# Threshold attention feeding a tanh-shrink layer: all queries and the second batch's masks turned on TensorE, first batch's weights three slots sooner

## The chip, the core and the metric

The kernel runs on one core of one Trainium2 chip. A core has five engines that run their own instruction streams and meet at semaphores: TensorE (PE in the profile, with its weight loads as PEld), VectorE (DVE), ScalarE (ACT), GpSimd (POOL) and SyncE (SP), which here only issues DMAs. The metric is the device time of one execution in microseconds.

## The reference

```python
def _attn_ref(q, k, v, tau):            # q, k, v: (8, 8, 576, 64) float32
    scores = matmul(q, k.T) / sqrt(64)
    thresh = max(scores, axis=-1) - tau          # tau = 0.02
    scores = where(scores >= thresh, scores, -1e9)
    attn = exp(scores - max(scores))
    attn = attn / (sum(attn) + 1e-9)
    return matmul(attn, v)
...
x = attn_out.transpose(0, 2, 1, 3).reshape(4608, 512)
h = x @ w_in                             # w_in: (512, 2048)
g = h - tanh(h)
out = g @ w_out                          # w_out: (2048, 512)
```

## The kernel before

**Tiles.** The 64 heads are taken as 32 pairs, four pairs to a batch entry ("batch" below). Each pair has nine score tiles of 128 query rows by 576 keys: kinds A and B (512 rows of each head, two A/B duos a head) and one tile M (j = 4), which holds the last 64 rows of both heads. Tile i is number j = i mod 9 of pair p = i div 9.

**Steps of a pair.** `load` brings k, q and v from DRAM through SP's queue. `split` (GpSimd, three operations) scales q or k by 256 and writes it as a float16 high and low half. `turn` transposes the halves: nine 128x128 transposes on TensorE into one of the two `ps_big` PSUM buffers, and one VectorE copy to SBUF; for k, two GpSimd copies then make the swapped `kS`. In the kernel before, `q_by_dma(p)` sends q of the odd pairs from 9 on (12 of them) through a DMA transpose on SP's queue instead. `split_v` (GpSimd, three casts) fills the value tile `vb`.

**Steps of a tile.** `scores` (four matmuls into `ps_big`, and one VectorE pass L323 that scales, copies and takes the row maximum), `shift` (a small VectorE operation L337 that makes the bias), `kink` (one ScalarE pass L357, a steep Prelu that sends what lies below the threshold far down, output `z`), `weights` (transposes z and takes the exponential, output `pT`), `attend` (matmuls with `vb` into `ps_o`), `norm` (VectorE), `emit_x` (transposes the normalised pair into the layer's input `xT`).

**Two ways to transpose z.** Where `on_pe(i)` holds, `weights` runs four or five 128x128 transposes on TensorE into PSUM (`psZ`) and one exponential per tile (512 or 640 wide, L386). Otherwise `kink` issues a DMA transpose on SP's queue for each finished duo or M tile (L365), into one of the `zt_pool` buffers, and `weights` runs one exponential of 1152 for the duo (L394). Before, TensorE does all tiles of pairs 0 to 3, tiles 0, 1, 4, 5, 6 of pairs 4 to 7, and none after.

**The layer.** `layers` gives the steps of a batch's 512 rows: `hidden` (four 512-wide matmuls, then `bend` = tanh on ScalarE and `shrink` on VectorE) and `project` (four 512-wide matmuls of a quarter of the sum). Steps are dealt out over the slots of the next batch's tiles, from its slot 4 to its last one; slots 0 to 3 of a batch have none. The first stage, over pairs 4 to 7, has 16 hidden steps and no projection; later ones have about one step a slot. The rest runs in a tail after the last tile.

**The order** is written out by hand, one loop over slots s. In slot s stand, in this order: `shift` and `scores` of tile s + AHEAD, `kink` of tile s + MASK, tanh, `weights` of tile s, the layer's steps, `attend` of tile s - LAG (2), `norm`, `emit_x`, and the steps of `PREP`, whose times are counted back from the slot in which a pair's first scores are due (`first = 9 p - AHEAD`). The casts of the layer's weights (16 pieces, GpSimd, L605) stand at every fourth score slot. Each engine keeps this order; the buffers' semaphores do the rest.

Of the kernel before, what the change touches and what calls it, by code (L numbers as in the profile page):

```python
# [9 lines left out]
F32 = mybir.dt.float32  # L10
BF16 = mybir.dt.bfloat16
FP16 = mybir.dt.float16
AX = mybir.AxisListType
ALU = mybir.AluOpType
# [4 lines left out]
def kernel(  # L19
# [11 lines left out]
    nc = tc.nc  # L31
    P = 128

    B, H, S, D = q.shape
# [6 lines left out]
    QKSC = 256.0  # L41
# [4 lines left out]
    HPAIR = H // 2  # L46
# [3 lines left out]
    TPP = 9  # L50
# [3 lines left out]

    def on_pe(i):
        p, j = divmod(i, TPP)
        return p < HPAIR or p < 2 * HPAIR and j in (0, 1, 4, 5, 6)

    W = 2 * S

    AHEAD = 8
    LDK = 16
    MASK = 5
    LAG = 2


# [45 lines left out]
    sc_pool = pool("sc", AHEAD - MASK + 2)  # L112
    st_pool = pool("st", 12)
    z_pool = pool("z", 4)
    zt_pool = pool("zt", 6)
    p_pool = pool("p", 3)
    o_pool = pool("o", 2)
    wt_pool = pool("wt", 2)
# [16 lines left out]
    def load(p, t):  # L135
        b, h0 = p // HPAIR, 2 * (p % HPAIR)
        hs = slice(h0, h0 + 2)
        src = {"k": k, "q": q, "v": v}[t]
        eng = nc.sync
        r = raws[p, t] = raw_pool.tile([P, 10, D], F32, name=f"{t}raw", tag=t)  # L140
        n = 8 if t == "v" else 10
        eng.dma_start(
            out=r[:, 0:n, :].rearrange("p (h c) d -> p h (c d)", h=2)[:, :, 0 : 4 * D],
            in_=src[b, hs, 0:512, :].rearrange("h (p c) d -> p h (c d)", c=4),
        )
        rem = src[b, hs, 512:S, :].rearrange("h s d -> s h d")
        if t == "v":
            eng.dma_start(out=r[0:64, 8:10, :], in_=rem)
        else:
            eng.dma_start(out=r[:, 4, :], in_=rem)  # L150

# [19 lines left out]
    hls = {}  # L171

    def split(p, t):
        x = raws.pop((p, t))[:, 0:9, :]
        hl = hl_pool.tile([P, TPP, 2, D], FP16, name=f"{t}hl", tag=t)
        nc.gpsimd.tensor_scalar(
            out=x, in0=x, scalar1=QKSC, scalar2=1.0, op0=ALU.mult, op1=ALU.mult
        )
        nc.gpsimd.tensor_copy(out=hl[:, :, 0, :], in_=x)
        nc.gpsimd.tensor_tensor(  # L180
            out=hl[:, :, 1, :], in0=x, in1=hl[:, :, 0, :], op=ALU.subtract
        )
        hls[p, t] = hl
# [22 lines left out]
    def split_v(p):  # L206
        r, vb = raws.pop((p, "v")), vbs[p % NV]
        nc.gpsimd.tensor_copy(
            out=vb[:, :, 0:4, 0:D],
            in_=r[:, 0:8, :].rearrange("p (h c) d -> p h c d", h=2),  # L210
        )
        nc.gpsimd.tensor_copy(out=vb[0:64, :, 4, 0:D], in_=r[0:64, 8:10, :])
        nc.gpsimd.tensor_copy(out=vb[64:P, :, 5, 0:D], in_=r[0:64, 8:10, :])

# [11 lines left out]
            out=out, lhsT=lhsT, rhs=rhs, is_transpose=True, start=True, stop=True  # L228
        )

    def q_by_dma(p):

        return p >= 2 * HPAIR and p % 2 == 1

    def turn(p, t):
        hl = hls.pop((p, t))
        if t == "q" and q_by_dma(p):
            m = mats[p, t] = qk_pool.tile([P, W], FP16, name=f"{t}T", tag=t)
            nc.sync.dma_start_transpose(
                out=m.rearrange("p (c r) -> p c r", c=TPP),  # L240
                in_=hl.rearrange("p c a d -> p (c a d)"),
            )
            return
        ps = ps_big.tile([P, W], FP16, name=f"ps_{t}", tag="big")
        for c in range(TPP):
            turn_chunk(
                ps[:, c * P : (c + 1) * P], c, hl[:, c, :, :].rearrange("p a d -> p (a d)")
            )
        m = qk_pool.tile([P, W], FP16, name=f"{t}T", tag=t)
        nc.vector.tensor_copy(out=m, in_=ps)  # L250
        mats[p, t] = m
        if t == "k":
            sw = qk_pool.tile([P, W], FP16, name="kS", tag="ks")
            for lo, hi in ((0, D), (D, 0)):
                o, i = sw[lo : lo + D, :], m[hi : hi + D, :]
                nc.gpsimd.tensor_copy(out=o, in_=i)  # L256
            mats[p, "ks"] = sw
# [31 lines left out]
    def scores(i):  # L289
        p, j = divmod(i, TPP)  # L290
        qT, kT, kS = mats[p, "q"], mats[p, "k"], mats[p, "ks"]
        ps = ps_big.tile([P, 1024], F32, name="psS", tag="big")
        main, rem, lo = slice(0, 512), slice(512, 576), 0
        if kind(j) == "B":
            main, rem, lo = slice(512, 1024), slice(448, 512), 448
        if j == 4:
            qrem = REM
            if q_by_dma(p):
                qrem = (slice(512, 640, 2), slice(513, 640, 2))
            for n, kk in enumerate((kT, kS)):  # L300
                for dst, srcs in ((main, MAIN), (rem, REM)):
                    for hh in range(2):
                        nc.tensor.matmul(  # L303
                            out=ps[64 * hh : 64 * hh + 64, dst],
                            lhsT=qT[:, qrem[hh]], rhs=kk[:, srcs[hh]],
                            start=(n == 0), stop=(n == 1),
                        )
        else:
            hh = int(j > 4)
            lhs = qT[:, j * P : (j + 1) * P]  # L310
            for n, kk in enumerate((kT, kS)):
                for dst, src in ((main, MAIN[hh]), (rem, REM[hh])):
                    nc.tensor.matmul(  # L313
                        out=ps[:, dst], lhsT=lhs, rhs=kk[:, src],
                        start=(n == 0), stop=(n == 1),
                    )
        sc = sc_pool.tile([P, S], F32, name="sc")
        if kind(j) == "B":
            mx = mxs[i] = mxs.pop(i - 1)
        else:  # L320
            mx = mxs[i] = st_pool.tile([P, 2], F32, name="mx", tag="mx")
        c = int(kind(j) == "B")
        nc.vector.tensor_scalar(  # L323
            out=sc, in0=ps[:, lo : lo + S], scalar1=SC, scalar2=None,
            op0=ALU.mult, op1=ALU.max, accum_out=mx[:, c : c + 1],
        )
        scs[i] = sc
# [279 lines left out]
    def w_load(piece):  # L607
# [17 lines left out]
        (8, lambda p: split(p, "k")),  # L625
        (7, lambda p: split(p, "q")),
        (5, lambda p: turn(p, "k")),
        (4, split_v),
    )

    plan = {}
    for p in range(1, NPAIR):
        first = TPP * p - AHEAD
        for d, f in PREP[3 if p == 1 else 0 :]:
            d -= p == 1 and d in (3, 5)
            plan.setdefault(first - d, []).append(lambda p=p, f=f: f(p))
        d = 5 if q_by_dma(p) else 3 - (p == 1)
        plan.setdefault(first - d, []).append(lambda p=p: turn(p, "q"))

    load(0, "v")  # L640
    for t in ("k", "q"):
# [15 lines left out]
        if at < -AHEAD:  # L657
            plan.setdefault(-AHEAD, []).extend(plan.pop(at))

    kinks = {}  # L660
    for i in range(NTILE):
        kinks.setdefault(i // 2 * 2 + 2 - AHEAD if i < 4 else i - MASK, []).append(i)
    for s in range(-AHEAD, NTILE + LAG + 3):
        p, j = divmod(max(s, 0), TPP)
        if 0 <= s < NTILE and j == 2 + LAG and p % HPAIR == 0 and p >= HPAIR:
            assert not todo
            todo = layers(stage, False)
            share = len(todo) / (HPAIR * TPP - 2 - LAG)
            done, stage = 0.0, stage + 1
        if 0 <= s + AHEAD - 1 < NTILE:  # L670
            shift(s + AHEAD - 1)
        if 0 <= s + AHEAD < NTILE:
            scores(s + AHEAD)
        if s == 1 - AHEAD:
            for t in ("k", "q", "ks"):
                turn_first(t, 1)
        for i in kinks.pop(s, []):
            kink(i)
        bend()
        if 0 <= s < NTILE:  # L680
            weights(s)
            if todo:
                done += share
                if j == TPP - 1 and p % HPAIR == HPAIR - 1:
                    done = 1e9
                while todo and done >= 1:
                    todo.pop(0)()
                    done -= 1
        if s == 0:
            nc.vector.tensor_tensor(  # L690
                out=fold, in0=ident_bf[:, 0:64], in1=ident_bf[:, 64:P], op=ALU.add
            )
        shrink()
        for store in stores[:-1]:
            store()
        del stores[:-1]
        if 0 <= s - LAG < NTILE:
            attend(s - LAG)
            pp, jj = divmod(s - LAG, TPP)
            if jj == 4:  # L700
                norm(pp, 0)
            if jj == 8:
                norm(pp, 1)
        pp, jj = divmod(s - LAG, TPP)
        if jj == 1 and 0 < pp <= NPAIR:
            emit_x(pp - 1)
        for step in plan.pop(s, []):
            step()
        if True:
            if s + AHEAD in w_when:  # L710
                if loaded:
                    w_cast()
                piece = next(pieces, None)
                if piece:
                    w_load(piece)
# [47 lines left out]
```

## Time and profile before

| | |
|---|---|
| median of 3 runs | 545.06 us (545.05 to 545.15) |
| the profiled execution | 545.06 us |
| its span in the trace | 542.9 us, so 2.2 us lie around it |
| granted TensorE clock, mean | 0.997 |
| busy: PE, DVE, ACT, POOL | 507.5, 447.1, 439.3, 290.7 us |
| first `hidden` matmul | 71.5 us |

The times of the prediction are sums against the profiled execution, which is the median. In the views, a line of a group is: source line, engine, operation, output<-input, shapes, count, then busy time, mean ns of one, and the idle time of the engine ahead of it. In the timeline each line is start, duration, engine, line, operation. A row of the table of windows gives, after the stretch and its length, busy time (and instructions) of PE, PEld, DVE, ACT and POOL, then the granted clock, the DMA share and GB/s.

### The profile page before, as it was taken

What the parts mean: (1) busy time and instruction counts of PE and PEld (TensorE: products, weight loads), DVE (VectorE), ACT (ScalarE), POOL (GpSimd) and SP (SyncE); (2) the same over time, 40 slices, a digit from 0 to 9 for tenths busy, and PEclk for the clock granted to TensorE, in tenths of its full rate; (3) what the DMA queues carried; (4) which work ended last, traced back from release to release, by engine and by line L of the source; (5) the groups of instructions that cost most, each with busy time, mean ns of one, the idle gap of its engine ahead of it and who ended that gap; (6) DMA issues with size and microseconds to landing.
All of it is one profiled execution on the core that took longest, in us unless ns stands there. A gap on an engine that the chain in (4) does not pass through costs nothing.

```text
span 542.9 us, 12962 instructions
## 1 busy us (share of the span) xinstructions
PE 507.5 (93%) x4722; PEld 290.3 (53%) x4790; DVE 447.1 (82%) x1196; ACT 439.3 (81%) x630; POOL 290.7 (54%) x390
## 2 busy tenths in 40 slices
PE   5888888889999899999999999999999999899997
PEld 3566655555555555555555555555555555444444
DVE  4999999898888899889988989989989988544440
ACT  4899999998898888889888989899888989633330
POOL 7899987765456666557555755666655730000000
PEclk9999999998999999999999999999999999999999
DMA  7554688679697988789988999999999965310103
GB/s 211 168 182 145 205 202 175 148 131 197 141 173 160 175 169 199 163 191 195 181 188 172 177 200 186 165 171 191 192 177 179 200 127 117 83 41 39 40 39 77
DMA packets 202239, 85.13 MB, mean 157 GB/s; under 512 B 169792, under 2 KB 194624, under 8 KB 202176
## 3 DMA queue, kind: packets, MB, share of 16 engines
q1 hardware_dynamic: 201584, 83.89, 72.7%
q8 instruction: 37, 0.61, 0.5%
q10 hardware_dynamic: 592, 0.43, 0.3%
q14 instruction: 26, 0.21, 0.1%
HBM read 36.70 MB, written 9.44 MB: 85 GB/s over the span
## 4 chain that ended last, share of the span: by engine, by line
PE 67%; DVE 19%; POOL 6%; ACT 4%; issue 3%; DMA 0%; ACTq 0%; SPq 0%; DVEq 0%; POOLq 0%
PE psY L504 19%; PE psH L478 17%; PE psS L313 14%; DVE sc L323 9%; PE psO L423 5%; DVE g L497 3%; PE psS L303 3%; PE ps_k L227 3%; PE psHt L478 3%; DVE nb L337 2%; ACT z L357 2%; DVE osb L438 1%; POOL kS L256 1%; PE ps_q L227 1%; PE psO L412 1%
## 5 line engine op out<-in xcount | busy, mean ns | idle before, releaser
L323 DVE TENSOR_SCALAR_CACHE_REDUCE sc<-psS 128x576 f32<-128x576 f32 x288 | 215.3, 749 | 16.4 <-PE psS L313 11.0
L357 ACT ACTIVATE z<-sc,nb 128x576 bf16<-128x576 f32 x256 | 194.2, 771 | 21.9 <-DVE nb L337 21.3
L256 POOL COPY kS<-kT 64x1152 f16<-64x1152 f16 x62 | 70.9, 1143 | 135.8 <-DVE nb L337 133.2
L504 PE MATMUL psY<-w_out_sb,g 128*128 128x512 bf16 (+1 forms) x556 | 138.4, 373 | 2.2 <-issue 0.8
L394 ACT ACTIVATE pT<-zT 128x1152 f16<-128x1152 bf16 (+1 forms) x128 | 137.3, 1073 | 0.0
L478 PE MATMUL psH<-xT,w_in_sb 128*128 128x512 bf16 x451 | 118.0, 379 | 6.5 <-DVE g L497 4.4
L313 PE MATMUL psS<-kT,qT 128*128 128x512 f16 (+1 forms) x512 | 105.6, 288 | 11.2 <-DVE sc L323 9.2
L491 ACT ACTIVATE th<-psH 128x512 f32<-128x512 f32 x128 | 75.5, 590 | 39.2 <-PE psH L478 37.0
L313 PEld LDWEIGHTS <-qT 128*128 128x128 f16 x1024 | 73.1, 98 | 61.3 <-issue 14.5
L497 DVE SCALAR_TENSOR_TENSOR g<-th,psH 128x512 bf16<-128x512 f32 x128 | 87.2, 681 | 18.4 <-ACT th L491 18.4
L313 PE MATMUL psS<-kS,qT 128*128 128x512 f16 x496 | 101.9, 287 | 0.1
L478 PEld LDWEIGHTS <-w_in_sb 128*128 128x128 bf16 x576 | 49.4, 98 | 60.7 <-issue 7.2
L504 PEld LDWEIGHTS <-g 128*128 128x128 bf16 x592 | 51.0, 98 | 56.6 <-issue 2.9
L423 PEld LDWEIGHTS <-pT 128*128 128x128 f16 x1280 | 55.7, 98 | 25.0 <-issue 1.4
L423 PE MATMUL psO<-vb,pT 128*128 128x65 bf16 x1280 | 61.5, 194 | 0.9 <-ACT pT L394 0.6
L337 DVE TENSOR_SCALAR nb<-mx 128x2 f32<-128x2 f32 (+1 forms) x160 | 49.1, 307 | 2.5
L386 ACT ACTIVATE pT<-psZ 128x640 f16<-128x640 bf16 (+1 forms) x56 | 37.6, 671 | 5.1 <-PE psZ L377 5.0
L180 POOL TENSOR_TENSOR qhl<-qraw,qhl 128x576 f16<-128x576 f32 x31 | 39.7, 1281 | 2.6
L180 POOL TENSOR_TENSOR khl<-kraw,khl 128x576 f16<-128x576 f32 x31 | 39.7, 1281 | 2.6
L250 DVE COPY kT<-ps_k 128x1152 f16<-128x1152 f16 x31 | 23.4, 756 | 13.6 <-PE ps_k L227 13.2
L514 DVE COPY yo<-psY 128x512 f32<-128x512 f32 (+1 forms) x31 | 21.1, 679 | 11.3 <-PE psY L504 6.4
L438 DVE TENSOR_TENSOR osb<-psO,rc 128x256 bf16<-128x256 f32 x64 | 27.2, 424 | 2.2
(77 smaller groups left out, 508.4 us busy)
## 6 DMA issues: line engine op xcount, KB each, us to landing
vraw<-in_v_dram SPq DMA_DIRECT2D x32, 256.0 KB, 3.4
out_dram<-yo SPq DMA_DIRECT2D x32, 256.0 KB, 3.0
kraw<-in_k_dram SPq DMA_DIRECT2D x31, 256.0 KB, 3.2
qraw<-in_q_dram SPq DMA_DIRECT2D x31, 256.0 KB, 3.6
wt<-in_moe_w_in_dram SPq DMA_DIRECT2D x8, 512.0 KB, 4.7
wt<-in_moe_w_out_dram SPq DMA_DIRECT2D x8, 512.0 KB, 4.1
zT<-z SPq DMA_TRANSPOSE x104, 3.5
kraw<-in_k_dram SPq DMA_DIRECT2D x32, 32.0 KB, 2.8
```

Of the source, the lines that this page charges most:

```text
L180: nc.gpsimd.tensor_tensor(out=hl[:, :, 1, :], in0=x, in1=hl[:, :, 0, :], op=ALU.subtract)
L256: nc.gpsimd.tensor_copy(out=o, in_=i)
L313: nc.tensor.matmul(out=ps[:, dst], lhsT=lhs, rhs=kk[:, src], start=(n == 0), stop=(n == 1),)
L323: nc.vector.tensor_scalar(out=sc, in0=ps[:, lo : lo + S], scalar1=SC, scalar2=None, op0=ALU.mult, op1=ALU.max, accum_out=mx[:, c : c + 1],)
L337: nc.vector.tensor_scalar(out=nb[:, 0:n], in0=mx[:, 0:n], scalar1=-1.0, scalar2=tau, op0=ALU.mult, op1=ALU.add,)
L357: nc.scalar.activation(out=z, in_=sc, func=ACT.Prelu, bias=nb, scale=1.0, alpha=STEEP)
L394: nc.scalar.activation(out=pt[:, 0 : n * P], in_=zts.pop(i)[:, 0:n, :], func=ACT.Exp)
L423: nc.tensor.matmul(out=po[:, (j - 1 - 5 * hh) + ab, :], lhsT=pt[:, blk * P : (blk + 1) * P], rhs=vb[:, hh, c, :], start=(n == 0), stop=(n ...
L478: nc.tensor.matmul(out=ps, lhsT=w_in_sb[:, c, n * P : (n + 1) * P], rhs=xs[m][:, c, :] if m < B else xR[:, c, :, :], start=(c == 0), stop= ...
L491: nc.scalar.activation(out=th, in_=ps, func=ACT.Tanh)
L497: nc.vector.scalar_tensor_tensor(out=gs[m][:, n, :], in0=th, scalar=-1.0, in1=ps, op0=ALU.mult, op1=ALU.add,)
L504: nc.tensor.matmul(out=ps, lhsT=gs[m][:, n, ms * P : (ms + 1) * P], rhs=w_out_sb[:, n, cols], start=(n == 0), stop=(n == DF_C - 1),)
```

## The change

- `on_pe(i)` now holds for all tiles of pairs 4 to 7 too: tiles 2, 3, 7 and 8 of each of them (eight duos) go from DMA transposes to TensorE.
- `q_by_dma` is gone: the 12 odd queries are turned on TensorE like the others, three slots ahead of their pair's first scores.
- AHEAD is 7 instead of 8, MASK 4 instead of 5, so a kink stands four slots ahead of its weights instead of five; scores still stand three slots ahead of the kink.
- Tiles of the first batch (i < 36) have `weights` and `attend` three slots sooner, at slots i - 3 and i - 1. Slots 33 to 35 have no weights. The layer still starts in slot 40.
- `split` writes its scaled float32 copy to a buffer of its own (`xs`), not over the loaded one; `load` brings the last 64 rows of v a second time for the upper partitions (32 more small DMAs on SP's queue); `zt_pool` has four buffers instead of six.

```diff
     def on_pe(i):
         p, j = divmod(i, TPP)
-        return p < HPAIR or p < 2 * HPAIR and j in (0, 1, 4, 5, 6)
+        return p < 2 * HPAIR
...
-    AHEAD = 8
+    AHEAD = 7
     LDK = 16
-    MASK = 5
+    MASK = 4
...
-    zt_pool = pool("zt", 6)
+    zt_pool = pool("zt", 4)
...
             eng.dma_start(out=r[0:64, 8:10, :], in_=rem)
+            eng.dma_start(out=r[64:P, 8:10, :], in_=rem)
...
-        x = raws.pop((p, t))[:, 0:9, :]
+        r = raws.pop((p, t))[:, 0:9, :]
+        x = hl_pool.tile([P, TPP, D], F32, name="xs", tag="xs")
         nc.gpsimd.tensor_scalar(
-            out=x, in0=x, scalar1=QKSC, scalar2=1.0, op0=ALU.mult, op1=ALU.mult
+            out=x, in0=r, scalar1=QKSC, scalar2=1.0, op0=ALU.mult, op1=ALU.mult
...
-        if t == "q" and q_by_dma(p):
-            m = mats[p, t] = qk_pool.tile([P, W], FP16, name=f"{t}T", tag=t)
-            nc.sync.dma_start_transpose(
-                out=m.rearrange("p (c r) -> p c r", c=TPP),
-                in_=hl.rearrange("p c a d -> p (c a d)"),
-            )
-            return
...
+        (3, lambda p: turn(p, "q")),
...
-        d = 5 if q_by_dma(p) else 3 - (p == 1)
-        plan.setdefault(first - d, []).append(lambda p=p: turn(p, "q"))
...
+    kinks, wts, atts = {}, {}, {}
+    for i in range(NTILE + 3):
+        at = i - 3 if i < HPAIR * TPP else i
+        atts.setdefault(at + LAG, []).append(i)
+        if i < NTILE:
+            wts.setdefault(at, []).append(i)
+            kinks.setdefault(i // 2 * 2 + 2 - AHEAD if i < 4 else i - MASK, []).append(i)
...
+        for i in wts.pop(s, []):
+            weights(i)
         if 0 <= s < NTILE:
-            weights(s)
```

More of the change, by code (lines that the diff above doesn't have):

```diff
@@ L212, in split_v @@
         nc.gpsimd.tensor_copy(out=vb[0:64, :, 4, 0:D], in_=r[0:64, 8:10, :])
-        nc.gpsimd.tensor_copy(out=vb[64:P, :, 5, 0:D], in_=r[0:64, 8:10, :])
+        nc.gpsimd.tensor_copy(out=vb[64:P, :, 5, 0:D], in_=r[64:P, 8:10, :])
     mats = {}
@@ L229, in turn_chunk @@
         )
-    def q_by_dma(p):
-        return p >= 2 * HPAIR and p % 2 == 1
     def turn(p, t):
         hl = hls.pop((p, t))
-        if t == "q" and q_by_dma(p):
-            m = mats[p, t] = qk_pool.tile([P, W], FP16, name=f"{t}T", tag=t)
-            nc.sync.dma_start_transpose(
-                out=m.rearrange("p (c r) -> p c r", c=TPP),
-                in_=hl.rearrange("p c a d -> p (c a d)"),
-            )
-            return
         ps = ps_big.tile([P, W], FP16, name=f"ps_{t}", tag="big")
@@ L296, in scores @@
         if j == 4:
-            qrem = REM
-            if q_by_dma(p):
-                qrem = (slice(512, 640, 2), slice(513, 640, 2))
             for n, kk in enumerate((kT, kS)):
@@ L304, in scores @@
                             out=ps[64 * hh : 64 * hh + 64, dst],
-                            lhsT=qT[:, qrem[hh]], rhs=kk[:, srcs[hh]],
+                            lhsT=qT[:, REM[hh]], rhs=kk[:, srcs[hh]],
                             start=(n == 0), stop=(n == 1),
@@ L658 @@
             plan.setdefault(-AHEAD, []).extend(plan.pop(at))
-    kinks = {}
-    for i in range(NTILE):
-        kinks.setdefault(i // 2 * 2 + 2 - AHEAD if i < 4 else i - MASK, []).append(i)
+    kinks, wts, atts = {}, {}, {}
[5 more added lines that the diff above has]
+            kinks.setdefault(i // 2 * 2 + 2 - AHEAD if i < 4 else i - MASK, []).append(i)
     for s in range(-AHEAD, NTILE + LAG + 3):
@@ L696 @@
         del stores[:-1]
[L697 to L706, printed above, removed]
+        for i in atts.pop(s, []):
+            pp, jj = divmod(i, TPP)
+            if i < NTILE:
+                attend(i)
+            if i < NTILE and jj in (4, 8):
+                norm(pp, int(jj > 4))
+            if jj == 1 and pp:
+                emit_x(pp - 1)
         for step in plan.pop(s, []):
```

## The prediction

> **What bounds the kernel now.** I read the page's busy rows and slices first, then the windows by stage, then the order of events on TensorE in a late stage, and last the waits of the transitions.
>
> ```profile
> PE 507.5 (93%) x4722; PEld 290.3 (53%) x4790; DVE 447.1 (82%) x1196; ACT 439.3 (81%) x630; POOL 290.7 (54%) x390
> PE   5888888889999899999999999999999999899997
> POOL 7899987765456666557555755666655730000000
> ```
>
> TensorE leads, but the slices show two regimes: up to some 75 us GpSimd is the full one. The windows say it in numbers:
>
> ```profile
> 30.00:40.00 10.00, 8.86 (x131) 6.55 (x130) 9.02 (x29) 9.64 (x17) 9.47 (x13) 1.00 0.63 202
> 101.50:116.00 14.50, 13.00 (x160) 8.56 (x159) 13.18 (x37) 13.43 (x22) 9.62 (x12) 1.00 0.50 109
> 305.00:363.00 58.00, 56.48 (x532) 31.75 (x540) 52.79 (x147) 52.02 (x72) 34.27 (x45) 1.00 0.98 183
> ```
>
> First batch (first row): PE has room (89%), ScalarE 96%, GpSimd 95%. First layer stage (second row, pairs 4 to 7): PE 90%, DVE 91%, ACT 93%, none alone. Later batches (third row): PE 97%, DVE 91%, ACT 90%. That a late PE is at its peak, and not only busy, is read from the starts:
>
> ```profile
> 194.93 0.67 PE L227 MATMUL ps_q<-ident_f,qhl 128*128 128x128 f16 x9
> 195.54 0.41 PE L313 MATMUL psS<-kT,qT 128*128 128x512 f16 x2
> 195.78 0.41 PE L313 MATMUL psS<-kS,qT 128*128 128x512 f16 x2
> 196.03 1.03 PE L478 MATMUL psH<-xT,w_in_sb 128*128 128x512 bf16 x4
> 196.89 0.48 PE L423 MATMUL psO<-vb,pT 128*128 128x65 bf16 x10
> 197.21 0.41 PE L313 MATMUL psS<-kT,qT 128*128 128x512 f16 x2
> ```
>
> From start to start a tile's scores take 0.49 us, a layer step 0.86, an attend 0.32, with nothing between. A later batch takes 58.26 us, the same in each (from one `emit_x` of a batch to the next batch's), and what PE idles of it, some 1.5 us of 58, lies mostly where slots have no layer step. So whatever is put on TensorE after pair 8 is paid. A slot there is 58.26/36 = 1.62 us.
>
> **The parts.**
>
> *Queries by TensorE (12 pairs).* Removed: 12 DMA transposes (1.3 to 1.4 us of SP's queue each). Added: 9 transposes and a copy of 0.75 us on VectorE (L250, 751 ns) each. The even pairs have this row: from the first transpose of a query to the next matmul 0.50 to 0.65 us, mean 0.57 (0.61 above). Eleven of the turns fall into slots with layer steps: 11 x 0.57 = 6.3. That of pair 9 falls into the end of the first layer stage, where VectorE is nearer to being the limit: 0.75. Sum **+7.0**. Cover for the copy is VectorE's 9% of idle time; if that failed, 12 x 0.75 = 9.0. Below: PE's 1.5 us of idle time a batch could swallow the two turns of a batch, so 0.
>
> The trace shows which transpose is the cheap one here: on TensorE 0.57 us of the full engine, by DMA none of it, and the exponentials and scores behind a DMA wait once in the whole run. The Trainium skill ("VectorE: DVE Perf Modes", "The three transpose paths" and its rules for authors) gives 390 ns for a 128x128 block on TensorE against 1309 ns by DMA, and advises TensorE where a PSUM destination will do. By that rule the change should not lose here, and the sum would be without the 7.0; it compares one block's latency, not what the fullest engine has left, and I go by the rows.
>
> *Eight duos of pairs 4 to 7 by TensorE.* Added: 72 transposes, and eight exponentials of 1152 become 512 and 640 wide. ScalarE is even: from one start to the next operation's, 1.06 us for 1152 and 0.48 + 0.58 for the pair. TensorE: four and five transposes take 0.24 and 0.29 us, so 8 x 0.53 = 4.2 us. PE idles 1.5 of 14.5 us a pair there and would come to 97%, with ACT and DVE above 90% and exponentials that wait for transposes of their own slot. I take half, **+2.1**; ends 0 (all in idle time) and 4.2.
>
> *The stall of pair 9.* The one place where a query by DMA came late:
>
> ```profile
> PE psS L313 <- DMA qT<-qhl: 1.5, 1, 1.5
> ...
> 120.00:122.00 2.00, 0.65 (x10) 0.22 (x6) 2.00 (x7) 2.00 (x4) 1.78 (x5) 1.00 0.46 120
> 122.00:124.00 2.00, 1.47 (x18) 0.90 (x19) 2.00 (x3) 1.77 (x3) 1.92 (x3) 0.99 1.16 261
> 124.00:126.00 2.00, 1.67 (x16) 1.11 (x16) 1.93 (x7) 2.00 (x3) 1.85 (x3) 0.50 0.78 148
> ```
>
> PE waits 1.5 us, and then the clock is 0.50 and 0.66 in the two windows from 124, some 1.7 us of PE's time. That goes: at most 3.2. But DVE shows 6.84 of 7 us busy from 121 to 128 (1.27 of it one L337 that ends with a GpSimd operation), so part would remain: **-1.5**, ends 0 and -3.2. What comes next there is VectorE.
>
> The Trainium skill ("TensorE: Matmul & The Clock Gate", Part 1) has the clock fall only after an idle window of about 3.4 us. PE's gaps here are 1.46 and 0.75 us and the clock still halves; by the rule the stall alone would count, 1.5 at most.
>
> *The front.* With AHEAD 7 the layer starts at score tile 47 instead of 48. In the first batch three pairs take 37.5 us (copies of kT at 35.73 and 73.26), 1.39 us a tile. GpSimd's operations follow each other there with gaps of 0.06 us, and their order against the scores is unchanged, so three slots sooner for weights doesn't hasten it; one tile less ahead of the layer does: -1.39, but its scores come back in the PE-bound part: +0.49. Exponentials of the first batch now also fill ScalarE's idle 3.3 us between 11.4 and 19 us, and around score tile 41 four of them (4 x 0.53 = 2.1 us) are already done; with DVE and POOL at 95% I count 0.7 of it. Sum **-1.6**, ends -0.9 and -3.
>
> *Kink to weights four slots instead of five*, for all pairs from 8 on. Tightest place of a late batch:
>
> ```profile
> 239.01 1.37 SPq L239 DMA_TRANSPOSE qT<-qhl  x1
> 241.86 1.40 SPq L365 DMA_TRANSPOSE zT<-z  x1
> 246.55 1.15 ACT L394 ACTIVATE pT<-zT 128x1152 f16<-128x1152 bf16 x1
> ```
>
> That transpose lands 3.9 us after its issue, at 245.8, so 0.8 us ahead of its exponential. One slot (1.62) less would leave -0.8; the query's DMA ahead of it in the queue goes (1.37) and a second v load comes (0.65): about -0.1. The next duo there has 1.3 us: about -0.3. Behind a late exponential stand the next kink and tanh on ScalarE, and `attend` two slots on. Some 0.4 us a batch reaches ScalarE, partly hidden in its 10%; six batches: **+0.7**, ends 0 and 6 (half a microsecond in two of four pairs, all paid).
>
> *Nothing:* SP's queue (50 of 58 us a batch; two transposes out, four small loads in); `xs` (the same three GpSimd operations); four zT buffers (three duos at most are between kink and exponential).
>
> Sum: 7.0 + 2.1 - 1.5 - 1.6 + 0.7 = +6.7; 545.06 + 6.7 = **551.8 us**.
>
> **Rivals.**
>
> *The first batch opens up, not slower.* If its pace is not GpSimd's but that of weights coming too late, then the slots would run at ScalarE's own 1.2 us (kink 0.67 + exponential 0.53) instead of 1.39: 36 x 0.19 = -6.8. With the first layer stage taking its transposes in idle time (2.1 less): 551.8 - 8.9 = 543. Decides if the first `hidden` matmul comes before 64 us. For: ScalarE 96% there. Against: GpSimd's gaps of 0.06 us from 18 to 84 us. Chance 0.10.
>
> *The shorter wait bites, clearly slower.* If late transposes hold ScalarE in each of the 24 late pairs by some 0.4 us, and tanh, and so the release of the layer's PSUM, comes later by as much: 24 x 0.4 = 9.6 in place of 0.7: 560. Decides from 0.25 us a pair on. For: 0.8 us of slack against a slot of 1.62. Against: ScalarE idles 1.5 us a pair. Chance 0.13.
>
> *The earlier weights do nothing*, since the layer's gate stays at slot 40: without the 0.7, 552.5, inside the forecast's own range.
>
> **How the numbers follow.** Forecast (548 to 556): 0.77; the rivals 0.10 and 0.13. The range of 8 in 10 goes from 546.5 to 557.5: the lower end has most of the queries' turns absorbed, the upper one a part of the second rival. What differs by more than 0.2% (1.1 us) can be told from no change. Of the first rival 0.07 is faster and 0.03 the same; a forecast that is off in every term adds 0.01 to the same: faster 0.07, same 0.04, slower 0.89.
>
> **What would show it.** Late batches of 59.4 us or more instead of 58.26, with PE at 97% or above and 31 VectorE copies of qT; the first `hidden` matmul near 70 us; pairs of the first layer stage at 14.9 us instead of 14.4; no half clock at 124 us; idle time ahead of L394 above 0.0 but under 5 us. Wrong, if late batches stay at 58.3 (the turns are hidden), if the first layer matmul comes before 64 us, or if ScalarE waits for zT by 6 us or more.

## The result, and the profile after

| | before | changed |
|---|---|---|
| median | 545.05 us (4 runs, 544.2 to 545.15) | 552.31 us (4 runs, 551.49 to 552.64) |
| profiled execution, its span | 545.06, 542.9 us | 552.06, 550.2 us |
| ratio of times | | 1.0134, 95% interval 1.0117 to 1.0152 |
| first `hidden` matmul | 71.5 us | 70.0 us |
| a late batch | 58.26 us | 59.4 us |

The change makes the kernel slower by 7.3 us. The page of the changed kernel, its busy rows and slices:

```profile
PE 517.8 (94%) x4901; PEld 303.3 (55%) x4970; DVE 453.0 (82%) x1208; ACT 440.5 (80%) x638; POOL 291.2 (53%) x390
PE   5899899989999999999999999999999999899996
POOL 7999987656456665556555656666655640000000
PEclk9999999999999999999999999999999999999999
```

TensorE has 10 us more work, VectorE 6, the others hardly any. GpSimd is full over the same first slices as before; the half clock after 124 us is gone (the tenth slice showed 8 before and shows 9). The place of pair 9, first in the kernel before, then in the changed one:

```profile
120.00:128.00 8.00, 5.71 (x54) 3.27 (x51) 7.84 (x20) 7.53 (x11) 5.87 (x9) 0.79 0.82 176
```
```profile
120.00:128.00 8.00, 6.40 (x77) 4.06 (x77) 7.27 (x20) 6.60 (x10) 7.21 (x10) 1.00 0.58 122
```

Between the matching `emit_x` of two batches, the table of windows has for the kernel before (first row), the changed one (second) and, ahead of its experiment, the kernel before with all queries on TensorE (third):

```profile
304.51:362.77 58.26, 56.74 (x537) 31.87 (x543) 53.05 (x146) 52.28 (x73) 34.53 (x45) 1.00 0.98 183
```
```profile
307.86:367.24 59.38, 58.04 (x554) 33.62 (x561) 53.84 (x151) 52.57 (x73) 34.55 (x45) 1.00 0.84 172
```
```profile
310.82:371.49 60.67, 58.19 (x555) 32.95 (x561) 54.95 (x148) 52.57 (x73) 34.46 (x45) 1.00 0.81 166
```

The changed kernel's late batch is 1.12 us longer, as long as two turns of 0.57 us. TensorE is busy 1.30 us more in it and idle 1.34 us, a little less than before (1.52). By stage, from the times of the last transpose of `emit_x` in the two traces: to the first `hidden` matmul -1.5; from there to the `emit_x` of pair 7 +2.2 (54.7 to 56.9); from there to that of pair 31 +6.0 (346.0 to 352.0); the tail after it +0.6. Together they are the span's +7.3. What the front gains is more than lost again by the end of pair 7.

The waits of ScalarE for z transposed by DMA, of which there were none, by the page's group:

```profile
L382 ACT ACTIVATE pT<-zT 128x1152 f16<-128x1152 bf16 (+1 forms) x120 | 128.0, 1066 | 2.3 <-DMA zT<-z 2.1
```

### The profile page after: what moved, and what is told of

It is laid out like the page before. It is cut to its first block, busy times and chain, and to the rows that moved or that the text cites. A ratio compares the mean times of both kernels' runs of the same rounds, so it can differ in the third digit from the quotient of the medians.

```text
span 550.2 us, 13368 instructions
## 1 busy us (share of the span) xinstructions
PE 517.8 (94%) x4901; PEld 303.3 (55%) x4970; DVE 453.0 (82%) x1208; ACT 440.5 (80%) x638; POOL 291.2 (53%) x390
## 4 chain that ended last, share of the span: by engine, by line
PE 76%; DVE 13%; ACT 6%; issue 3%; DMA 1%; SPq 0%; ACTq 0%; DVEq 0%
PE psY L492 21%; PE psH L466 18%; PE psS L301 17%; PE psO L411 5%; DVE sc L311 5%; PE psS L291 3%; ACT pT L374 3%; PE psHt L466 2%; ACT z L345 2%; PE ps_q L229 2%; PE ps_k L229 2%; DVE g L485 2%; DVE yo L502 2%; PE psZ L365 1%; PE psO L400 1%
## 5 line engine op out<-in xcount | busy, mean ns | idle before, releaser
L247 POOL COPY kS<-kT 64x1152 f16<-64x1152 f16 x62 | 70.9, 1143 | 142.7 <-DVE nb L325 141.1
L382 ACT ACTIVATE pT<-zT 128x1152 f16<-128x1152 bf16 (+1 forms) x120 | 128.0, 1066 | 2.3 <-DMA zT<-z 2.1
L301 PEld LDWEIGHTS <-qT 128*128 128x128 f16 x1024 | 75.5, 98 | 67.4 <-issue 13.6
L374 ACT ACTIVATE pT<-psZ 128x640 f16<-128x640 bf16 (+1 forms) x72 | 47.1, 655 | 7.4 <-PE psZ L365 7.0
L325 DVE TENSOR_SCALAR nb<-mx 128x2 f32<-128x2 f32 (+1 forms) x160 | 46.0, 288 | 0.9
L182 POOL TENSOR_TENSOR qhl<-xs,qhl 128x576 f16<-128x576 f32 x31 | 39.7, 1282 | 2.6
L182 POOL TENSOR_TENSOR khl<-xs,khl 128x576 f16<-128x576 f32 x31 | 39.7, 1281 | 2.6
L241 DVE COPY qT<-ps_q 128x1152 f16<-128x1152 f16 x31 | 23.4, 756 | 9.8 <-PE ps_q L229 9.8
L365 PE MATMUL psZ<-ident_bf,z 128*128 128x128 bf16 x288 | 26.7, 219 | 4.0 <-ACT pT L374 2.7
```

Source lines behind the costliest of these rows:

```text
L182: nc.gpsimd.tensor_tensor(out=hl[:, :, 1, :], in0=x, in1=hl[:, :, 0, :], op=ALU.subtract)
L301: nc.tensor.matmul(out=ps[:, dst], lhsT=lhs, rhs=kk[:, src], start=(n == 0), stop=(n == 1),)
L374: nc.scalar.activation(out=pt[:, off * P : (off + n) * P], in_=ps[:, 0 : n * P], func=ACT.Exp)
L382: nc.scalar.activation(out=pt[:, 0 : n * P], in_=zts.pop(i)[:, 0:n, :], func=ACT.Exp)
```

## Experiments

Each ran five rounds beside the kernel before (medians 545.17 to 545.52 there). "8/5" stands for AHEAD 8 and MASK 5, and so on.

**1. The changed kernel with the odd queries by DMA.**

```diff
+    def q_by_dma(p):
+        return p >= 2 * HPAIR and p % 2 == 1
...
-        (3, lambda p: turn(p, "q")),
...
+        d = 5 if q_by_dma(p) else 3 - (p == 1)
+        plan.setdefault(first - d, []).append(lambda p=p: turn(p, "q"))
```

> The changed kernel with one part undone: the 12 odd queries go by DMA transpose again, five slots ahead of their pair. The sum's theory (a turn on TensorE costs 0.57 us of a full engine, and the stall of pair 9 comes back): 552.3 - 7.0 + 1.5 = 546.8 us, late batches at 58.3 us instead of 59.4. Rival (the shorter wait between kink and weights is what costs): the queries give back under 2 us, 550.5 or more, late batches stay near 59.4.

Measured: 552.86 us (551.34 to 555.92), no gain over 552.31; late batches 59.3 to 60.9. The sum's theory misses, though TensorE has 12 turns less. Its waits from 130 to 470 us, engine and line, what it waited for, total, times, longest:

```profile
ACT pT L395 <- DMA zT<-z: 12.3, 13, 2.6
...
PEld L424 <- ACT pT L395: 5.0, 7, 1.9
```

The exponentials now wait for z, and the attends for them. So undoing this part alone brings a new cost with it; whether queries by DMA need the longer wait is tested in runs 6 and 9.

**2. The duos of pairs 4 to 7 by DMA again.**

```diff
-        return p < 2 * HPAIR
+        return p < HPAIR or p < 2 * HPAIR and j in (0, 1, 4, 5, 6)
```

> The changed kernel with tiles 2, 3, 7 and 8 of pairs 4 to 7 by DMA transposes again. The sum's theory (half of 4.2 us of transposes is paid in the first layer stage): 552.3 - 2.1 = 550.2 us. Rival A (they lie in TensorE's idle time): 552.3, no difference. Rival B (all paid): 548.1.

Measured: 553.08 us (551.93 to 554.52). Rival A: undoing them gives nothing back that the time of the whole can show, neither 4.2 us nor half of it, in a stage where TensorE idled 10%. The traces are a little finer: with the duos on TensorE the stage from the first `hidden` matmul to the `emit_x` of pair 7 takes 56.9 us, by DMA 55.9, but the first `hidden` matmul comes at 70.0 against 70.6 us. By the end of pair 7 the duos on TensorE are 0.4 us behind, in one trace each.

**3. The first batch's weights in their later slots.**

```diff
-        at = i - 3 if i < HPAIR * TPP else i
+        at = i
```

> The changed kernel with the first batch's weights and attends at slots i and i + 2, as for the others. The sum's theory (GpSimd sets the first batch's pace, the earlier weights bring 0.7 us): 553.0 us. Rival A (late weights set that pace): 559 us. Rival B (they bring nothing, since the layer's gate is at slot 40): 552.3.

Measured: 552.4 us (552.13 to 552.89); first `hidden` matmul at 70.2 us against 70.0. Rival B: the earlier weights bring nothing measurable, and the first batch did not open up. Whether GpSimd's pace or the gate at slot 40 makes them useless is not separated.

**4. AHEAD and MASK back.**

```diff
-    AHEAD = 7
+    AHEAD = 8
...
-    MASK = 4
+    MASK = 5
```

> The changed kernel with AHEAD 8 and MASK 5 again, the first batch's weights still three slots ahead of their number, four zT buffers kept. The sum's theory: one score tile more ahead of the layer +0.9, the kink-to-weights slot given back -0.7, so 552.5 us. Rival (the shorter wait holds ScalarE by 0.4 us in each of 24 pairs): 543 to 545 us.

Measured: 556.95 us (556.57 to 558.24), late batches 60.7. Neither theory: the step that I had at +0.2 is worth 4.6 us, and in the other direction than the rival had it. With queries on TensorE the lower pair of constants is a gain. It lies in the later batches: 357.0 us from the `emit_x` of pair 7 to that of pair 31, against 352.0.

**5. The kernel before with all queries on TensorE.**

```diff
-        return p >= 2 * HPAIR and p % 2 == 1
+        return False
```

> The kernel before with one part done alone: no query goes by DMA, all 31 are turned on TensorE three slots ahead, AHEAD 8 and MASK 5 kept. The sum's theory (0.57 us a turn, stall of pair 9 gone): 545.5 + 7.0 - 1.5 = 551 us, late batches 59.4 us. Place theory, formed on the run with AHEAD 8 (late batches of 60.7 us there; a turn in slot 7 of a pair stands right behind the norm of the first head on VectorE and costs 1.2 us): 545.5 + 12 x 1.2 - 1.5 = 558 us, late batches 60.7.

Measured: 557.49 us (557.49 to 557.95), +12.3 over 545.17; late batches 60.7. Twelve turns cost nearly twice what the sum has. Of the 2.41 us that a late batch is longer, TensorE is busy for 1.45 and idle for 0.96 (third row of the table of windows above: 60.67 - 58.19 = 2.48 us idle, against 1.52). TensorE's waits in late stages (186 to 470 us), first the kernel before, then this one, then the changed kernel:

```profile
PE psH L478 <- DVE g L497: 3.0, 5, 0.7
PE psS L313 <- DVE sc L323: 1.6, 5, 0.7
...
PE psH L478 <- DVE xT L468: 0.5, 1, 0.5
```
```profile
PE psS L313 <- DVE sc L323: 5.0, 14, 0.6
PE psH L478 <- DVE xT L468: 2.2, 4, 0.5
PE psH L478 <- DVE g L497: 1.6, 5, 0.3
```
```profile
PE psS L301 <- DVE qT L241: 1.8, 5, 0.4
PE psH L466 <- DVE g L485: 1.6, 5, 0.3
PE psY L492 <- issue: 0.6, 4, 0.2
PE psS L301 <- DVE sc L311: 0.2, 1, 0.2
```

In the second the scores wait for VectorE 14 times. The timeline at one of them:

```profile
364.24 0.19 DVE L437 RECIPROCAL rc<-psO 128x5 f32<-128x5 f32 x1
364.46 0.42 DVE L438 TENSOR_TENSOR osb<-psO,rc 128x256 bf16<-128x256 f32 x1
...
364.80 0.34 DVE L443 SCALAR_TENSOR_TENSOR osb<-psO,rc,own 128x128 bf16<-128x128 f32 x1
364.96 0.67 PE L227 MATMUL ps_q<-ident_f,qhl 128*128 128x128 f16 x9
365.06 0.75 DVE L323 TENSOR_SCALAR_CACHE_REDUCE sc<-psS 128x576 f32<-128x576 f32 x1
...
365.73 0.75 DVE L250 COPY qT<-ps_q 128x1152 f16<-128x1152 f16 x1
365.87 0.41 PE L313 MATMUL psS<-kT,qT 128*128 128x512 f16 x2 [0.24 <-DVE sc L323]
```

The turn stands one slot behind the first head's norm. VectorE is still at the norm, so the pass that frees the other `ps_big` buffer comes late, and the next scores find both buffers taken: one by a tile, one by the query. This is one of the 14; that the place of the turn makes the whole excess is not shown by it (run 7 tests it).

**6. The changed kernel with queries by DMA and 8/5.** The edits of 1 and 4 together.

> The changed kernel with two parts undone together: odd queries by DMA again, and AHEAD 8, MASK 5. If the pair of them is the whole loss (the query's transposes need the longer wait, and the shorter wait needs the queries off the DMA queue): 545 to 546.5 us, no wait of exponentials for zT, late batches 58.3. If the duos of pairs 4 to 7, the second v load or the buffers cost anything: 547 or more. Single undoings added up (-0 for the queries, +4.6 for AHEAD and MASK) would give 557.

Measured: 546.88 us (546.23 to 548.12); ratio to before 1.0025, interval 1.0014 to 1.0035; most late batches 58.26, waits for zT 1.0 us. The queries' way and AHEAD with MASK are nearly the whole loss, together. The duos, the earlier weights, the second v load and the buffers are left with +1.4 (1.0014 to 1.0035 of 545 us is 0.8 to 1.9). In the trace 0.6 us of it is there by the end of pair 7: the first `hidden` matmul comes 1.0 us sooner than in the kernel before, and the stage up to the `emit_x` of pair 7 takes 56.2 us instead of 54.7. Which of the five edits does this is not separated.

**7. 8/5 with the queries' turn one slot later.**

```diff
-        (3, lambda p: turn(p, "q")),
+        (2, lambda p: turn(p, "q")),
...
-            d -= p == 1 and d in (3, 5)
+            d -= p == 1 and d in (2, 5)
```
on top of the edit of 4.

> The changed kernel with AHEAD 8, MASK 5 and the turn of every query one slot later (two slots ahead of the pair's first scores, so in slot 8 of a pair, where the changed kernel has it with AHEAD 7). Place theory: most of the 4.6 us that AHEAD 8 cost come back, 552 to 554 us, late batches near 59.4. Rival (it is the longer run-ahead or wait itself that costs): 556 to 558, late batches at 60.7.

Measured: 555.2 us (554.52 to 555.87), late batches 60.2. The turn's own place gives 1.75 of the 4.64 us back, less than the 3 to 5 that the place theory had. TensorE still waits 3.3 us for the scores' pass and 2.2 us for `xT`; the turn of k and the pair's other steps stand a slot differently too, and these were not separated.

**8. The odd queries' transposes made twice.**

```diff
-        for c in range(TPP):
+        odd_q = t == "q" and p >= 2 * HPAIR and p % 2 == 1
+        for c in [*range(TPP)] * (2 if odd_q else 1):
```

> The changed kernel with the nine transposes of each of the 12 odd queries made twice, into the same buffer; the VectorE copy stays single. TensorE is the bound there (the sum's theory): 12 x 0.5 to 0.57 = +6 to +6.8, so 558 to 559 us, late batches 60.4 to 60.5. Rival (the VectorE copy, or the place among the scores, is what a turn costs): under +2, 554 or less.

Measured: 560.79 us (560.66 to 562.09), late batches 60.95: +8.5 in all, 0.71 us a turn. In a late batch, 1.57 us longer, TensorE is busy 0.86 us more and idle 0.71 us more (2.05 against 1.34). TensorE's time is paid in full and brings more waits with it; that the copy or the place is the whole price of a turn is out.

**9. Queries by DMA, 8/4.** The edit of 1, and AHEAD alone back to 8.

> The changed kernel with odd queries by DMA, AHEAD 8 and MASK 4: against the run with queries by DMA and 8 and 5 (546.9 us) one slot less between kink and weights alone, the turns in the same slots. Wait theory (four slots are too few once the query's transposes stand in SP's queue too): 551 to 553 us, exponentials wait for zT about 10 us. Rival (the new places that come with AHEAD 7 cost the 6 us of the run with 7 and 4): 547 to 548, waits for zT under 2 us.

Measured: 555.19 us (555.08 to 555.28), +8.3 over 8/5, worse than the theory's own figure. The edit does a little more than the expectation says: the kink stands one slot further behind its scores, too, and the pool of score tiles has six buffers instead of five. Waits from 186 to 470 us:

```profile
ACT pT L395 <- DMA zT<-z: 29.0, 19, 2.4
```

**10. Queries on TensorE, 8/4.** AHEAD alone back to 8.

> The changed kernel with AHEAD 8 and MASK 4, all queries on TensorE: between the run with 8 and 5 (557.0) and the changed kernel with 7 and 4 (552.3). If AHEAD, that is the slots in which turns and scores stand against the layer's steps, is what gave the 4.6 us: 556 to 557.5, late batches near 60.7. If MASK, the shorter way from kink to weights, is: 552 to 553.5, late batches near 59.4.

Measured: 557.05 us (556.78 to 557.89), late batches 60.7, as with 8/5.

Its waits over the same stretch have nearly none for zT (0.3 us); the scores' waits for VectorE stay:

```profile
PE psS L301 <- DVE sc L311: 5.1, 14, 0.6
```

The six runs make a table (median, and in brackets what exponentials waited for zT from 186 to 470 us):

| | 8/5 | 8/4 | 7/4 |
|---|---|---|---|
| odd queries by DMA | 546.9 (1.0) | 555.2 (29.0) | 552.9 (12.3) |
| all on TensorE | 557.0 (0.0) | 557.1 (0.3) | 552.3 (2.1) |

With AHEAD 8, MASK 4 instead of 5 matters only where queries go by DMA (+8.3). With MASK 4, AHEAD 7 instead of 8 gives -4.7 with queries on TensorE; by DMA it gives -2.3, little more than the scatter of run 1 (551.3 to 555.9). AHEAD 7 with MASK 5 was not run.

**11 and 12. More queries by DMA.** The kernel before with every query from pair 10 on by DMA, and the same with 9/6.

```diff
-        return p >= 2 * HPAIR and p % 2 == 1
+        return p >= 2 * HPAIR + 2
```

> The kernel before with all queries from pair 10 on by DMA (22 instead of 12), AHEAD 8 and MASK 5. By the price of a turn on TensorE (0.57 us of PE to 1.0 us as measured in the kernel before): 11 even ones less, 545.2 - 6 to -11 = 534 to 539 us, late batches 56 to 57. Rival (SP's queue, 50 of 58 us, takes two more transposes a batch and the z transposes come late): 546 to 552, with exponentials that wait for zT by 8 us or more.

Measured: 544.43 us (542.59 to 547.65); ratio 0.9987, interval 0.9969 to 1.0004: it can't be told from the kernel before, and lies between the two theories. Late batches are 57.8 to 58.7 us. What the turns free comes back as a new wait (186 to 470 us):

```profile
PEld L313 <- DMA qT<-qhl: 6.5, 8, 1.8
...
PE psS L313 <- DMA qT<-qhl: 2.9, 3, 1.4
...
ACT pT L394 <- DMA zT<-z: 2.6, 3, 1.6
```

> The same with AHEAD 9 and MASK 6, so that the transposes of z have one slot more. If the run with 8 and 5 waits for zT, this gives it back: 535 to 541 us. If that one does not wait, this costs one more score tile ahead of the layer, +1 us over it.

Measured: 551.29 us (548.79 to 554.95). The first `hidden` matmul comes at 75.9 us instead of 71.3, and the waits for queries stay (5.3 and 4.2 us). No version here beats the kernel before clearly.

## Why the prediction was right, and where its steps were not

The time (551.8 forecast, 552.3 measured) and the late batch (59.4 forecast, 59.4 measured) came out; several steps of the sum did not, and they offset each other.

- *Queries by TensorE, +7.0, with the stall at -1.5.* Done alone it is +12.3 (run 5), where these two terms make +5.5, and 9.0 was named as the worst. TensorE's own part is priced about right: run 8 pays 0.71 us a turn for nine more transposes, against 0.57. What failed is the sentence that VectorE's 9% of idle time covers the turn: in the kernel before, the turn stands right behind the norm, and the scores' waits for VectorE grow from 1.6 to 5.0 us over 284 us. I read VectorE's idle share of a batch where the slot decides. How much of the excess is due to that place is open: one slot later gave 1.75 us back (run 7).
- *AHEAD, -0.9 of the front's -1.6, and MASK, +0.7.* Together I had -0.2; with queries on TensorE they are worth -4.6 (run 4). The front itself moved about as forecast (first `hidden` matmul at 70.0 instead of 71.5 us), but not by AHEAD: in the runs with the change's other edits it comes at 70.0 to 70.8 us with AHEAD 7 and at 70.0 to 70.9 with AHEAD 8, and in runs 5 and 11, made from the kernel before, at 71.7 and 71.3. So the -1.39 for one tile less did not show, and what made the front shorter among the other edits stays open. I looked for what AHEAD does at the front and not for where it puts the steps of `PREP`, which are counted from it, against the layer's and the norm's slots in every batch. In a late batch this is where the 1.2 us a turn of run 5 fall back to 0.56 (60.67 to 59.38 us for the batch). Part of it is the query's turn (1.75 us, run 7); the rest stays open.
- *MASK, +0.7 with an end of 6.* With queries on TensorE and AHEAD 8 it is nothing (run 10). The second rival's mechanism is real, but only where queries go by DMA: 29 us of waits and +8.3 (run 9). The change avoids it because it takes the queries off SP's queue in the same step: 2.1 us of waits in all from 186 to 470 us. My line "about -0.1" for the tightest transpose had the right reason.
- *Eight duos, +2.1, and the earlier weights, -0.7.* Both nothing that the whole time could show (runs 2 and 3). TensorE's idle time covered the duos all or nearly (0.4 us is left by the end of pair 7 in the traces of run 2). The weights did nothing, as the third rival had it; its reason was not tested.
- *The stall of pair 9, -1.5.* It and the half clock are gone; its worth alone was not measured. The half clock cost TensorE less than the 1.7 us put down for it: half of the 1.67 us that it was busy from 124 to 126 us and 0.34 of the 1.93 us after that, 1.5 in all. That VectorE comes next there holds: in runs 4 and 5, without the stall, scores wait at the same place for VectorE's pass, 1.18 and 0.84 us.
- *Nothing for the rest:* run 6 leaves +1.4 for five edits together, two of which are the ones above. With queries on TensorE the same five come to -0.5 (run 4 against run 5), which can't be told from nothing.

Put in order: +12.3 for the queries, -0.5 for the duos, weights, v load and buffers on top (run 5 against run 4), -4.6 for AHEAD with MASK: 545.17 + 7.14 = 552.31. Against my steps that is +6.8, -1.9 and -4.4: together 0.5. So the total was right in part by luck, and so was the late batch: with AHEAD and MASK as before it would have been 60.7 us (run 4). What was argued rightly is that TensorE's own work on a turn is paid there; that it waits for nothing more is due to AHEAD, which I had not seen.

## What to carry to other kernels

Undoing one part of a change measures that part only if no other part leans on it: here each of two parts, undone alone, gave nothing or a loss, and both together gave nearly all. When a constant from which other steps are counted is moved by one, list what else moves with it and what stands in the new slot on the engine next to the bound. An engine's idle share over a batch says little of whether it is free in the one slot where it is needed.

## What the runs showed of the hardware

- In the 14 traces of this case TensorE's granted clock halved only twice between 20 and 530 us: in the kernel before from 124 us (0.99, 0.50 and 0.66 in the 2 us windows from 122) and in run 9 from 368 us (0.55 and 0.60 in the two from there). Both make about 3.4 us at half clock. These are the 3.41 us ahead of each fall, and a later stretch of run 9 that no fall followed:

```profile
120.53:123.94 3.41, 1.59 (x20) 0.90 (x19) 3.41 (x7) 3.18 (x5) 3.17 (x5) 1.00 0.94 222
```
```profile
364.79:368.20 3.41, 1.59 (x20) 0.84 (x17) 2.96 (x12) 1.57 (x3) 3.17 (x5) 1.00 1.09 215
426.20:429.61 3.41, 2.03 (x22) 1.06 (x20) 3.31 (x12) 1.89 (x3) 3.20 (x5) 1.00 1.10 151
```

  The Trainium skill ("TensorE: Matmul & The Clock Gate", Part 1) has the clock fall after an idle window of about 3.4 us. The length agrees with these rows, but the window need not be without work: TensorE was busy for 47% of it (1.59 of 3.41 us), and no single gap was over 1.6 us. With 60% (2.03 of 3.41 us) the clock stayed. So the prediction read the rule too narrowly when it set it against single gaps.
- One slot (1.6 us) less between the issue of a DMA transpose and its use turned 1.0 us of waits into 29.0 us over 284 us, single waits of up to 2.4 us, where two queries a batch stood in the same queue, and 0.0 into 0.3 us where they didn't (runs 6, 9, 4 and 10). SP's queue was busy some 50 of 58 us in run 9 and 45 in run 10.
